# A new hand-written order for a gated attention and expert kernel: single output matmuls, squares moved between engines, stores and copies at other places

## The chip, the cores and the metric

The kernel runs on one NeuronCore of a Trainium2 chip. The core has five engines that run side by side and meet through semaphores: TensorE (PE, matmuls; its weight loads, PEld, overlap them), VectorE (DVE), ScalarE (ACT), GpSimd (POOL) and SyncE (SP, which here only issues DMAs). The metric is the device time of one execution in microseconds (us). Before the change the median of three runs is 221.41 us (220.65 to 221.46).

## The reference, cut to what matters

Inputs are x (8 batches, 8 heads, 512 rows, 64 columns), state (8, 8, 32, 64), w_in (512 x 2048), w_out (2048 x 512) and alpha (2048). Per batch and head two cross attentions are made, then a layer with the activation h + sin(alpha h)^2 / alpha runs over all rows:

```python
scores = scale * x @ state.T;   a = softmax(scores);   xread = a @ state
scores2 = scale * state @ x.T;  a2 = softmax(scores2); sread = a2 @ x
rows = concat([xread, sread], axis=2)        # 544 rows a batch, heads side by side: 4352 x 512
h = rows @ w_in
s = sin(alpha * h)
g = h + s * s / (alpha + 1e-9)
out = g @ w_out                              # 4352 x 512, float32
```

Inside, matmul operands are bfloat16; the sums are float32.

## The kernel before, in words

**Tiles.** The 512 rows of x of one batch are one unit t = 0 to 7; the 256 rows of all the state reads are a ninth unit, t = 8. The 2048 columns between the two big matmuls are cut into 16 tiles f of 128. `xread @ w_in` is not made in two steps: for each batch the kernel first makes M = state @ w_in per head (`m`, in four slices s and two head groups g, each a PSUM tile that `me` copies out as bfloat16), and then h = A M, where A is the softmax (`h`: two 512-column matmuls per f; for the first batch `hg`, one matmul of the two each). For t = 8 `h` is four 256-column matmuls on `xs_all`.

**One f tile.** `h` fills a PSUM bank; `si` (ScalarE) takes the sine; `sq` squares it, on ScalarE (A), VectorE (V) or GpSimd (G); `gt` (VectorE) adds h and frees the bank, leaving the tile gT. Then `o` multiplies gT with a tile of w_out into the output tile of 128 rows `st` (four per batch, 16 matmuls of 512 columns in each). `oc` copies the finished output tile to an `o_sb` buffer (six of them), `os` stores it from SP's queue.

**The attention of a batch.** `lx` loads x of a batch as bfloat16, issued by GpSimd; `pk` (VectorE, in two halves) copies it into another arrangement; `td` transposes it by a DMA on SP's queue (for batch 1, `xt` on TensorE); `sc` makes the scores, `ex` the exponent, `rs`, `rr` sum and reciprocal, `nm` (GpSimd) the product A, `ad` transposes A by DMA on SP's queue into AT, which `h` needs. `w`, `cs`, `rc`, `xs` make the state's read into `xs_all`. A change between exponent and sine makes ScalarE load a table.

**Loads at the start.** x of batch 0 comes in four parts by SP (`lq`); GpSimd issues state (`l_st`), w_in in four parts (`li`), w_out in four (`lo`) and x of the next batches (`lx`).

**What sets the order.** Nothing is scheduled by a machine: `ORDER` (lines 21 to 155) is a list of step names, and the kernel calls the method of each in turn, under a manual schedule. So each engine runs its own instructions in the order of that list, and each DMA queue too; a step that must wait holds up whatever stands behind it on its engine. The parts of a step's name are its arguments: `sq.3.7.V` is batch 3, f 7, on VectorE; `o.0.3.2.3` is batch 0, output rows 3, f from 2 up to 3. The order also names the PSUM bank of each tile (`h.1.2.5`: bank 5). The eight banks hold one tile each, so a tile in a bank can start only when the reader of the last one is done. `warm_up` steps are matmuls on zeros that no result uses.

The loop that plays the list is

```python
for step in ORDER:
    name, *args = step.split(".")
    getattr(steps, name)(*(int(a) if a.isdigit() else a for a in args))
```

Of the kernel before, what the change touches and what calls it, by code (L numbers as in the profile page):

```python
# [13 lines left out]
FP32 = mybir.dt.float32  # L14
# [31 lines left out]
si.0.12 o.0.0.10.11 o.0.3.9.11 sq.0.13.G ad.1 hg.0.15.0.2 sq.0.12.A o.0.1.10.12 hg.0.15.1 gt.0.12
o.0.2.8.10 si.0.15 o.0.2.10.11 gt.0.13 o.0.0.11.12 hg.0.14.0.4 sq.0.15.A hg.0.14.1 o.0.3.11.13
si.0.14 gt.0.15 o.0.0.12.13 o.0.1.12.13 o.0.3.13.14 sq.0.14.A pk.2.0.V o.0.1.13.14 pk.2.1.V h.1.2.5
gt.0.14 h.1.4.6 td.2 si.1.2 lx.3.0.1 h.1.0.2 si.1.4 o.0.0.13.15 sq.1.2.V h.1.1.4 si.1.0 gt.1.2
sq.1.4.G o.0.3.14.16 si.1.1 o.0.2.11.13 sq.1.0.A oc.0.3.V h.1.6.5 sq.1.1.G gt.1.4 o.0.2.13.14 os.0.3  # L50
h.1.3.0 si.1.6 gt.1.0 o.0.1.14.16 si.1.3 sq.1.6.G h.1.13.6 gt.1.1 oc.0.1.A o.0.2.14.15 o.0.0.15.16
si.1.13 h.1.15.2 sq.1.3.G lx.4.0.1 gt.1.6 os.0.1 o.0.2.15.16 oc.0.0.A h.1.5.4 sq.1.13.V oc.0.2.V
si.1.15 h.1.7.3 os.0.0 gt.1.3 o.1.1.0.1.5 si.1.5 os.0.2 h.1.8.1 sq.1.15.G gt.1.13 o.1.1.1.2 si.1.7
o.1.2.0.2.7 sq.1.5.A o.1.1.2.3 sq.1.7.G h.1.12.0 gt.1.15 si.1.8 h.1.9.6 gt.1.5 o.1.2.2.3 si.1.12
sq.1.8.G o.1.2.3.5 gt.1.7 si.1.9 o.1.1.3.4 h.1.10.2 sq.1.12.A pk.3.1.V h.1.11.4 sq.1.9.G gt.1.8
o.1.2.5.6 si.1.10 o.1.2.6.7 gt.1.12 h.1.14.3 si.1.11 sq.1.10.G o.1.2.7.8 gt.1.9 sc.2.1.1 si.1.14
o.1.1.4.7 sq.1.11.A pk.3.0.V sq.1.14.G o.1.1.7.8 gt.1.10 td.3 o.1.2.8.9 sc.2.0.0 o.1.1.8.9 gt.1.11
o.1.1.9.10 ex.2.0 o.1.3.0.2.6 gt.1.14 o.1.3.2.4 o.1.2.9.10 o.1.3.4.5 o.1.2.10.12 ex.2.1 o.1.2.12.13
rs.2.0 o.1.1.10.11 m.2.2.2.4.3.0 rr.2.0 rs.2.1 o.1.2.13.14 nm.2.0.0.4.G me.2.3.0.A o.1.2.14.15 w.0.1
rr.2.1 me.2.2.1.A me.2.3.1.V o.1.3.5.6 nm.2.1.0.4.G me.2.2.0.A o.1.3.6.7 o.1.2.15.16 cs.0 oc.1.2.A  # L60
m.2.0.3.4.0.2 ad.2 rc.0 o.1.3.7.8 me.2.1.1.A o.1.3.8.9 sc.3.0.7 xs.0.1 me.2.1.0.A o.1.1.11.12 os.1.2
me.2.0.0.V sc.3.1.2 me.2.0.1.A o.1.1.12.13 o.1.3.9.10 xs.0.0 pk.4.1.V pk.4.0.V td.4 o.1.3.10.11
ex.3.0 o.1.1.13.16 ex.3.1 rs.3.0 o.1.3.11.13 oc.1.1.A o.1.3.13.14 rr.3.0 h.2.0.0 rs.3.1 nm.3.0.0.4.G
os.1.1 o.1.3.14.16 si.2.0 rr.3.1 h.2.1.3 oc.1.3.V nm.3.1.0.4.G h.2.2.4 h.2.8.1 os.1.3 h.2.3.7 ad.3
si.2.2 o.1.0.0.3.2 si.2.8 sq.2.0.V o.1.0.3.4 sq.2.2.G gt.2.0 h.2.4.5 si.2.1 o.1.0.4.6 si.2.3
sq.2.8.G o.1.0.6.7 gt.2.2 h.2.9.6 si.2.4 o.2.3.0.1.0 o.1.0.7.8 sq.2.1.G o.1.0.8.9 sq.2.3.A gt.2.8
o.1.0.9.10 h.2.5.4 si.2.9 gt.2.3 o.1.0.10.11 sq.2.4.G o.1.0.11.12 si.2.5 h.2.7.1 gt.2.1 o.1.0.12.13
sq.2.9.A sq.2.5.G o.1.0.13.14 gt.2.4 o.1.0.14.15 si.2.7 o.1.0.15.16 o.2.0.0.1.7 gt.2.9 o.2.0.1.2
oc.1.0.A h.2.6.3 sq.2.7.G gt.2.5 o.2.3.1.2 os.1.0 o.2.3.2.3 si.2.6 h.2.10.5 o.2.3.3.4 sq.2.6.A
# [88 lines left out]
class Steps:  # L158
# [372 lines left out]
    def h(k, t, f, bank):  # L531
# [9 lines left out]
        else:  # L541
            for q in range(k.Q):
# [3 lines left out]
                )  # L546


    def hg(k, t, f, g, *bank):
        if g == 0:  # L550
            k.t["h", t, f] = k.ps(bank[0], [k.P, k.S], FP32, "h_ps")
        k.nc.tensor.matmul(  # L552
# [28 lines left out]
    def o(k, t, st, f0, f1, *bank, half=None):  # L581
        cols = k.cols(half)
# [81 lines left out]
```

## Time and profile before

| | |
|---|---|
| median of the runs | 221.41 us |
| the profiled execution | 221.22 us, span 219.2 us |
| PE busy | 211.4 us, 96% |
| VectorE busy | 162.9 us, 74% |
| ScalarE busy | 173.4 us, 79% |
| GpSimd busy | 106.2 us, 48% |
| chain that ended last | PE 90%, DMA 6% |
| `gt` (L576), 512 columns | 128 times, mean 742 ns |
| `si` (L560), 512 columns | 128 times, mean 695 ns |
| square on GpSimd / ScalarE / VectorE (L201, L569, L201) | mean 1045 / 640 / 449 ns |
| `pk` (L348) | 14 times, mean 429 ns |
| x loads (L275) | 7, median 7.5 us from issue to landing |

The page and the trace come from one execution. Times in it count from the start of its span. A duration is longer than an instruction's share of its engine, since the next one starts before the last has drained; where it matters, the distance from start to start is named. Idle time of an engine that the last chain does not run through costs nothing.

### The profile page before, as it was taken

The page shows a single profiled execution, that of the slowest core. Times are in us where ns is not written, and L with a number is a line of the kernel's source. Part 1 is how long each engine was busy: PE and PEld are TensorE (multiplying, and loading weights), DVE is VectorE, ACT ScalarE, POOL GpSimd, SP SyncE. Part 2 cuts the span into 40 slices and gives each one's busy share as a digit, 9 for nine tenths or more (in the row PEclk, how much of TensorE's full clock was granted, in tenths as well). Part 3 has the DMA queues.
Part 4 walks back from the last instruction along what each step waited for, and adds up shares of the span by engine and source line. Part 5 has one row for each costly group of instructions (what it writes and reads, how often), then busy time and mean ns, then how long its engine had stood idle before and what let it go on. Part 6 is the DMA issues. An engine that isn't in the chain of part 4 may idle for free.

```text
span 219.2 us, 4303 instructions
## 1 busy us (share of the span) xinstructions
PE 211.4 (96%) x1593; PEld 104.5 (48%) x1619; DVE 162.9 (74%) x287; ACT 173.4 (79%) x297; POOL 106.2 (48%) x114
## 2 busy tenths in 40 slices
PE   7989999999999999999999999999999999999994
PEld 3744544444444534444454444454445555665452
DVE  3769996999787789989888788888667987661201
ACT  4799778997998979898996999798848896785111
POOL 5959533895195647753943387273501082121000
PEclk9999999999999999999999999999999999999999
DMA  6999999987491029167145327470220211012042
GB/s 195 178 206 204 205 204 146 217 169 133 101 238 48 3 92 143 57 144 96 48 79 131 109 71 96 134 110 0 48 100 0 98 48 48 0 51 96 1 143 96
DMA packets 38052, 23.48 MB, mean 107 GB/s; under 512 B 20992, under 2 KB 33680, under 8 KB 38032
## 3 DMA queue, kind: packets, MB, share of 16 engines
q1 hardware_dynamic: 26128, 15.08, 26.5%
q0 software_dynamic: 11648, 8.13, 26.0%
q8 instruction: 12, 0.20, 0.3%
q14 instruction: 8, 0.07, 0.1%
q10 hardware_dynamic: 256, 0.01, 0.1%
HBM read 17.44 MB, written 8.91 MB: 120 GB/s over the span
## 4 chain that ended last, share of the span: by engine, by line
PE 90%; DMA 6%; POOL 1%; issue 1%; ACT 0%
PE o_ps L587 54%; PE h_ps L537 22%; DMA w_in_sb<-in_moe_w_in_dram 5%; PE m_ps L488 4%; PE h_ps L543 3%; PE h_ps L552 2%; PE w_ps L450 2%; PE s_ps L399 2%; PE w_ps L461 1%; DMA s<-in_state_dram 1%; POOL w_in_sb L282 1%; PE x_ps L376 0%; POOL st_nat L267 0%; POOL s01b L255 0%; ACT o_sb L595 0%
## 5 line engine op out<-in xcount | busy, mean ns | idle before, releaser
L587 PE MATMUL o_ps<-w_out_sb,gT 128*128 128x512 bf16 (+2 forms) x542 | 133.9, 373 | 1.6 <-issue 1.0
L576 DVE SCALAR_TENSOR_TENSOR gT<-s,inva_sb,h_ps 128x512 bf16<-128x512 bf16 (+1 forms) x144 | 96.8, 713 | 20.4 <-POOL s L201 10.8
L201 POOL TENSOR_TENSOR s<-s 128x512 bf16<-128x512 bf16 (+1 forms) x75 | 75.9, 1022 | 64.4 <-ACT s L560 62.7
L560 ACT ACTIVATE s<-h_ps,alpha_sb 128x512 bf16<-128x512 f32 (+1 forms) x144 | 88.8, 670 | 11.1 <-PE h_ps L543 4.5
L587 PEld LDWEIGHTS <-gT 128*128 128x128 bf16 x560 | 52.3, 98 | 60.3 <-issue 5.0
L537 PE MATMUL h_ps<-AT,M 128*128 128x512 bf16 x219 | 60.0, 379 | 0.3
L537 PEld LDWEIGHTS <-M 128*128 128x128 bf16 x224 | 21.7, 98 | 25.9 <-issue 0.4
L569 ACT ACTIVATE s<-s 128x512 bf16<-128x512 bf16 (+1 forms) x53 | 31.4, 594 | 0.8
L201 POOL TENSOR_TENSOR A<-E,rR 128x512 bf16<-128x512 bf16 x16 | 16.6, 1056 | 23.8 <-ACT o_sb L595 12.9
L595 ACT COPY o_sb<-o_ps 128x512 f32<-128x512 f32 (+2 forms) x24 | 13.7, 570 | 16.6 <-PE o_ps L587 16.5
L496 ACT CAST M<-m_ps 128x512 bf16<-128x512 f32 x35 | 18.6, 594 | 8.2 <-PE m_ps L488 8.2
L496 DVE CAST M<-m_ps 128x512 bf16<-128x512 f32 x29 | 18.9, 679 | 2.5 <-PE m_ps L488 2.1
L595 DVE COPY o_sb<-o_ps 128x512 f32<-128x512 f32 x11 | 7.5, 685 | 12.9 <-PE o_ps L587 12.9
L201 DVE TENSOR_TENSOR s<-s 128x512 bf16<-128x512 bf16 (+1 forms) x16 | 7.0, 439 | 6.2 <-ACT s L560 6.1
L410 DVE TENSOR_REDUCE R<-E 128x16 f32<-128x512 bf16 x16 | 10.4, 657 | 0.7 <-ACT E L406 0.6
L488 PE MATMUL m_ps<-w_in_sb,stT 64*32 64x512 bf16 x256 | 10.2, 382 | 0.1
L468 DVE RECIPROCAL rC<-w_ps 128x128 f32<-128x128 f32 x8 | 7.6, 948 | 3.3 <-PE w_ps L461 3.2
L303 PE MATMUL warm_ps<-warm 128*128 128x128 bf16 (+3 forms) x66 | 8.6, 271 | 1.4 <-DVE warm L209 1.2
L552 PE MATMUL h_ps<-AT,M 128*128 128x512 bf16 x29 | 8.4, 379 | 0.9 <-ACT M L496 0.7
L406 ACT ACTIVATE E<-s_ps 128x512 bf16<-128x512 f32 x16 | 8.8, 602 | 0.4 <-PE s_ps L399 0.4
L543 PE MATMUL h_ps<-xs_all,w_in_sb 128*128 128x256 bf16 x64 | 9.1, 273 | 0.0
L543 PEld LDWEIGHTS <-w_in_sb 128*128 128x128 bf16 x64 | 6.3, 98 | 3.4
(56 smaller groups left out, 101.8 us busy)
## 6 DMA issues: line engine op xcount, KB each, us to landing
out_dram<-o_sb SPq DMA_DIRECT2D x33, 256.0 KB, 2.3
xnat<-in_x_dram POOLq DMA_DIRECT2D x7, 512.0 KB, 7.5
w_in_sb<-in_moe_w_in_dram POOLq DMA_DIRECT2D x4, 512.0 KB, 10.9
w_out_sb<-in_moe_w_out_dram POOLq DMA_DIRECT2D x4, 512.0 KB, 18.0
x<-in_x_dram SPq DMA_DIRECT2D x4, 256.0 KB, 4.2
st_nat<-in_state_dram POOLq DMA_DIRECT2D x1, 256.0 KB, 5.3
out_dram<-o_sb SPq DMA_DIRECT2D x1, 192.0 KB, 1.9
s<-in_state_dram SPq DMA_DIRECT2D x1, 128.0 KB, 2.2
```

The lines of the kernel that those rows point to most:

```text
L201: {"V": k.nc.vector, "G": k.nc.gpsimd}[eng].tensor_tensor(out, a, b, ALU.mult)
L410: k.nc.vector.reduce_sum(R[:, g], k.t["E", b][:, g].rearrange("p c (h j) -> p (c h) j", j=k.Ns), axis=AX.X)
L488: k.nc.tensor.matmul(k.t["m", b, s + n, g][o0:o0 + k.Ns, :], k.stT[k.half(r), b * k.G + g, c0:c0 + k.Ns], k.w_in_sb[k.half(r), 2 * g + h, ...
L496: k.copy(eng)(k.t["M", b][:, g, s * k.FW:(s + 1) * k.FW], k.t["m", b, s, g][:])
L537: k.nc.tensor.matmul(hp[:, :n], k.t["M", t][:, g, fs], k.t["AT", t][:, g, :], start=(g == 0), stop=(g == k.G - 1),)
L543: k.nc.tensor.matmul(hp[:, :n], k.w_in_sb[:, q, fs], k.xs_all[:, q].rearrange("p b j -> p (b j)"), start=(q == 0), stop=(q == k.Q - 1),)
L552: k.nc.tensor.matmul(k.t["h", t, f][:], k.t["M", t][:, g, f * k.P:(f + 1) * k.P], k.t["AT", t][:, g, :], start=(g == 0), stop=(g == k.G - 1),)
L560: k.nc.scalar.activation(s[:, :n], k.t["h", t, f][:, :n], ACT.Sin, scale=k.alpha_sb[:, f:f + 1])
L569: k.nc.scalar.activation(s2[:, :n], s[:, :n], ACT.Square)
L576: k.nc.vector.scalar_tensor_tensor(gT[:, :n], k.t["s2", t, f][:, :n], k.inva_sb[:, f:f + 1], k.t["h", t, f][:, :n], ALU.mult, ALU.add,)
L587: k.nc.tensor.matmul(k.t["o", t, st, half][:, cols], k.t["gT", t, f][:, rows], k.w_out_sb[:, f, cols], start=(f == 0), stop=(f == k.FT - 1),)
L595: k.copy(eng)(o_sb[:, cols], k.t["o", t, st, half][:, cols])
```

## The change

The list is replaced as a whole by another order of the same work, and two methods are cut finer so that the list can say more. `hg` no longer takes a bank: `ho` takes it, and the two matmuls of a tile can come in either order. `o` is one matmul, and `oo` takes its bank; the 16 matmuls of an output tile can come in any order of f, each tile's first matmul starts the sum and its 16th ends it (`k.made` counts them). `m` steps are listed one slice at a time.

What the list changes besides, counted from the two lists: squares go from 53 / 16 / 75 on ScalarE / VectorE / GpSimd to 46 / 55 / 43; copies of M (`me`) from 35 / 29 on ScalarE / VectorE to 38 / 26; three of the four casts of batch 0's x (`xq`) from ScalarE to VectorE; the warm-up matmuls from 66 to 15. The stores `os` stand at other places of SP's queue, some well behind their `oc`: `os.1.0` to `os.1.3` come in one run behind `os.2.3`. The two halves of `pk` are apart for most batches, and `pk.3.1.V` and `pk.5.1.V` stand earlier among VectorE's steps. The last piece of the output is `oh.7.3.0` (384 columns) instead of `oh.7.3.1` (128 columns).

```diff
@@ the order (before): its start, the steps around pk.3 and pk.5, its end
-touch_x l_s01 consts touch lq.0.S ident_ l_alpha lq.1.S zero.0 warm_up.7.512.3 exp_table lq.2.S
...
-sq.1.8.G o.1.2.3.5 gt.1.7 si.1.9 o.1.1.3.4 h.1.10.2 sq.1.12.A pk.3.1.V h.1.11.4 sq.1.9.G gt.1.8
...
-os.2.2 h.3.3.0 gt.3.4 oc.2.1.A h.3.12.2 si.3.3 pk.5.1.V o.3.2.0.1.7 os.2.1 m.4.2.1.3.5.6 pk.5.0.V
...
-oc.7.0.A o.7.2.2.5 os.7.0 o.7.2.5.11 oh.7.3.0.1 o.7.2.11.13 och.7.3.0.A o.7.2.13.15 osh.7.3.0
-o.7.2.15.16 oh.7.3.1.4 oc.7.2.V os.7.2 och.7.3.1.A osh.7.3.1
@@ the order (after): its start, the steps around pk.3.1 and pk.5.1, the stores of batch 1, its end
+touch_x l_s01 consts touch lq.0.S ident_ l_alpha lq.1.S zero.0 warm_up.5.512.7 exp_table lq.2.S
...
+o.0.2.13 o.0.0.13 o.0.0.14 o.0.0.15 pk.1.1.V o.0.3.13 o.0.1.14 oo.1.3.1 lx.3.0.1 h.1.0.5 oc.0.0.A
+si.1.0 pk.2.0.V h.1.14.6 o.0.3.15 si.1.14 o.0.2.14 o.0.2.15 oc.0.2.A h.1.6.0 si.1.6 sq.1.14.G
+pk.2.1.V td.2 oc.0.3.V sq.1.6.G o.0.1.13 o.0.1.15 oc.0.1.A os.0.1 h.1.4.4 si.1.4 h.1.7.2 si.1.7
+sq.1.7.G oo.1.2.7 sq.1.0.V gt.1.0 o.1.3.0 o.1.2.0 pk.3.1.V h.1.9.3 h.1.2.5 gt.1.14 o.1.2.14 o.1.3.14
...
+si.3.14 sq.3.14.V gt.3.14 o.2.0.3 h.3.10.2 si.3.10 sq.3.10.A gt.3.10 gt.3.8 o.2.2.13 lx.5.0.1
+pk.5.1.V o.2.2.8 o.2.2.2 h.3.0.5 si.3.0 sq.3.0.V o.2.2.3 h.3.11.0 si.3.11 o.2.0.7 o.2.0.8 oc.2.0.A
...
+sq.3.11.A gt.3.11 gt.3.6 si.3.12 sq.3.12.G o.2.1.4 gt.3.12 o.2.1.1 h.3.5.4 o.2.1.3 os.1.1 os.1.2
+h.3.2.5 os.1.3 o.3.3.15 os.1.0 si.3.5 sq.3.5.G gt.3.5 o.2.2.1 si.3.2 h.3.3.0 si.3.3 sq.3.3.G ad.4
...
+oc.8.0.V os.8.0 o.7.2.15 o.7.1.0 o.7.2.11 o.7.2.8 o.7.2.13 o.7.2.7 oh.7.3.1.0 o.7.2.0 o.7.2.6
+och.7.3.1.V oc.7.2.V os.7.2 o.7.1.1 o.7.1.3 o.7.1.15 oc.7.1.A os.7.1 oh.7.3.0.0 osh.7.3.1
+och.7.3.0.A osh.7.3.0
@@ the methods
-        k.t = {}
+        k.t, k.made = {}, {}
...
-    def hg(k, t, f, g, *bank):
-        if g == 0:
-            k.t["h", t, f] = k.ps(bank[0], [k.P, k.S], FP32, "h_ps")
+    def ho(k, t, f, bank):
+        k.t["h", t, f] = k.ps(bank, [k.P, k.S], FP32, "h_ps")
+        k.made["h", t, f] = 0
+
+    def hg(k, t, f, g):
+        k.made["h", t, f] += 1
         k.nc.tensor.matmul(
             k.t["h", t, f][:], k.t["M", t][:, g, f * k.P:(f + 1) * k.P], k.t["AT", t][:, g, :],
-            start=(g == 0), stop=(g == k.G - 1),
+            start=k.made["h", t, f] == 1, stop=k.made["h", t, f] == k.G,
         )
...
-    def o(k, t, st, f0, f1, *bank, half=None):
+    def oo(k, t, st, bank, half=None):
+        k.t["o", t, st, half] = k.ps(bank, [k.P, k.DOUT], FP32, "o_ps")
+        k.made["o", t, st, half] = 0
+
+    def o(k, t, st, f, half=None):
         cols = k.cols(half)
-        if f0 == 0:
-            k.t["o", t, st, half] = k.ps(bank[0], [k.P, k.DOUT], FP32, "o_ps")
         rows = slice(st * k.P, (st + 1) * k.P) if t < k.B else slice(st, k.B * k.Ns, 2)
-        for f in range(f0, f1):
-            k.nc.tensor.matmul(
-                k.t["o", t, st, half][:, cols], k.t["gT", t, f][:, rows],
-                k.w_out_sb[:, f, cols], start=(f == 0), stop=(f == k.FT - 1),
-            )
+        k.made["o", t, st, half] += 1
+        k.nc.tensor.matmul(
+            k.t["o", t, st, half][:, cols], k.t["gT", t, f][:, rows], k.w_out_sb[:, f, cols],
+            start=k.made["o", t, st, half] == 1, stop=k.made["o", t, st, half] == k.FT,
+        )
...
     def oh(k, t, st, half, bank):
-        k.o(t, st, 0, k.FT, bank, half=half)
+        k.oo(t, st, bank, half=half)
+        for f in range(k.FT):
+            k.o(t, st, f, half=half)
```

## The prediction

> **What bounds the kernel now.** I read the page first (share of each engine, chain that ended last), then the busy times by stretch, then who waits for whom, then the loads one by one.
>
> ```profile
> span 219.2 us, 4303 instructions
> PE 211.4 (96%) x1593; PEld 104.5 (48%) x1619; DVE 162.9 (74%) x287; ACT 173.4 (79%) x297; POOL 106.2 (48%) x114
> ...
> PE 90%; DMA 6%; POOL 1%; issue 1%; ACT 0%
> ```
>
> TensorE (PE) is busy in 96% of the span and 90% of the chain that ended last. The 6% of DMA is the wait for the third part of w_in at the start. By stretch (columns: length, then busy time and count of PE, weight loads, VectorE, ScalarE, GpSimd):
>
> ```profile
> 0.00:17.40 17.40, 14.71 (x186) 8.76 (x187) 9.86 (x25) 12.77 (x23) 12.59 (x22) 1.00 1.01 194
> ...
> 216.00:219.20 3.20, 0.12 (x3) 0.00 (x0) 0.00 (x0) 0.27 (x1) 0.00 (x0) 1.00 0.31 110
> ...
> 17.40:216.00 198.60, 196.53 (x1407) 95.78 (x1432) 153.04 (x263) 160.41 (x274) 93.62 (x93) 1.00 0.49 99
> ```
>
> From 17.4 us, when that part lands, to 216 us PE is busy for 196.5 of 198.6 us. Asked what PE waited for from 20 to 216 us, the trace names one thing:
>
> ```profile
> PE o_ps L587 <- issue: 1.0, 6, 0.2
> ```
>
> So no other engine holds PE up now. The time is a head of 17.4 us set by DMA, a PE part with almost nothing to win, and a tail of 3.2 us. The profiled execution took 221.22 us for its span of 219.2; the median of the runs shown is 221.41 (220.65 to 221.46). My sum is made against 221.22.
>
> **The change part by part.** *TensorE's work.* The matmuls are the same but for warm-ups (66 before, 15 after), which lie in the head. I add the steps of either order from the first `m` on w_in's third part (17.4 us) with what the trace shows from start to start: 216 ns for a 512-column matmul, 0.325 us for an `m` pair of tiles, 0.24 `sc`, 0.46 `xt` and `w`, 0.30 `cs`. Before: 776 full matmuls and the rest, end at 214.9 (the trace: 216.1; 17 stretches of `m` with some 0.09 us at each turn are not in it). After: 773 and the same rest. Three `hg` matmuls more stand ahead of that `m`, in a stretch where PE waits for w_in anyway: **-0.65 us**. Bounds: 0 if `hg` comes late there, -0.65 if all three fit. I take -0.65, since `m` for w_in's first part starts at 11.87 and 11 `hg` need 2.4 of the 5.5 us up to 17.4. The runs of adjacent `m` steps number 17 in both orders, so splitting the `m` steps costs nothing.
>
> *Single matmuls instead of runs, started in any order* (`ho`, `oo`, `o` with one f): each matmul has its own weight load in both kernels (98 ns beside 216), so nothing by itself; the present trace already holds `o_ps` and `h_ps` matmuls taking turns at 216 ns.
>
> *The tail.* The last piece was 128 columns (matmul 219 ns, copy 265, 64 KB store 1.8 us). It becomes the 384-column piece (326, 478, 192 KB 1.9 us): **+0.4 us**.
>
> *The head.* Three of four x casts go from ScalarE (618 ns each) to VectorE, `inva` comes later, warm-ups thin out. All of it lies before the first `m` at 11.87 us, which waits for w_in (issued behind the same GpSimd steps in both orders): nothing; a chain late by one cast, 0.6 us, would still leave 2.5 us of room up to 17.4.
>
> *Squares.* GpSimd does 43 instead of 75, VectorE 55 instead of 16, ScalarE 46 instead of 53. VectorE gains 35 full squares at 0.345 us from start to start (12.1), 4 half ones (0.8), three x casts (about 1.3), and loses three `me` (1.8): about +13 us beside 45.6 us of idle time from 17.4 to 216. Its total is not the bound. GpSimd loses 32 us and ScalarE some 4, off the path.
>
> ```profile
> L201 DVE TENSOR_TENSOR s<-s x16: 285/424/658, 15.1 to 192.4; 128x512 bf16<-128x512 bf16 x15, 128x256 bf16<-128x256 bf16 x1
>   POOL s L201: 10.8, 24
> ```
>
> Of 15 full squares on VectorE two (578 and 658 ns) ran longer beside a GpSimd step. With 2 in 15 of 39 added ones, that is 5 times 0.2 us, 1 us of VectorE's time and none of PE's unless it falls at a tight place; on the other side VectorE's 10.8 us of waits behind GpSimd's squares shrink. Zero on PE's path, bounds 0 and +1.
>
> [...]
>
> *Where x loads meet VectorE.* This is what I hold decisive. `lx.b` is issued by GpSimd, `pk.b` copies the landed tile on VectorE, in order with the `gt` steps that PE needs. Issues and, in order, the microseconds from issue to landing of each:
>
> ```profile
> 33.97 0.94 POOL L275 DMA_DIRECT2D xnat<-in_x_dram  x1
> 43.36 0.94 POOL L275 DMA_DIRECT2D xnat<-in_x_dram  x1
> ...
> 81.50 0.94 POOL L275 DMA_DIRECT2D xnat<-in_x_dram  x1
> ...
> 98.94 0.94 POOL L275 DMA_DIRECT2D xnat<-in_x_dram  x1
> ```
> ```profile
> xnat<-in_x_dram POOLq DMA_DIRECT2D x1, 512.0 KB, 7.3
> xnat<-in_x_dram POOLq DMA_DIRECT2D x1, 512.0 KB, 8.2
> xnat<-in_x_dram POOLq DMA_DIRECT2D x1, 512.0 KB, 7.5
> xnat<-in_x_dram POOLq DMA_DIRECT2D x1, 512.0 KB, 5.6
> ```
> ```profile
> 47.51 0.41 DVE L348 COPY xp<-xnat 128x1024 bf16<-128x1024 bf16 x1
> ...
> 92.74 0.75 DVE L348 COPY xp<-xnat 128x1024 bf16<-128x1024 bf16 x2
> ```
>
> A load alone takes 5.6 us; beside a DMA transpose 7.3 and 7.5, beside stores 8.2. Today the copies come 13.5 us (batch 3) and 11.2 us (batch 5) after the issue, so nothing waits. The new order pulls both forward:
>
> - Batch 3: `lx.3` follows `sq.0.15.G`. PE's sum ends `h.0.15` at 32.3, ScalarE's sine after it takes 0.9, the square 1.0: issue at 34.3. `pk.3.1.V` now stands right behind `gt.1.0`: `h.1.0` ends at 37.8, sine 0.9, VectorE's `oc.0.3`, square and `gt` bring it to 40.2. The landing goes as in the same place now (7.3, beside `td.2`): 41.6. Behind it waits `gt.1.14`, and PE wants it for `o.1.2.14` at 41.9 (101 full matmuls after 17.4, and 2.7 us of others). Landing plus copy 0.34, `gt` 0.74 and 0.1 of signals is 42.8: **+0.9 us**. At 5.6 us the load lands at 39.9 and costs nothing; at 8.2 it costs 1.8.
> - Batch 5: `sc.4.1` ends at 77.4; exponent 0.8, sum and reciprocal 0.9, two GpSimd products 2.1: `lx.5` at 81.3, as now. But `pk.5.1.V` moves from behind `gt.3.4` to behind `gt.3.10` and `gt.3.8`, which VectorE ends at 86.7. Beside the load stand five stores in one run (`os.2.3`, then `os.1.1`, `1.2`, `1.3`, `1.0`, held behind it on SP's queue) and `ad.4`. The nearest row is the load beside stores, 8.2: landing at 89.5. Behind the copy wait `sq.3.0`, `gt.3.0`; PE's `h.3.2.5` at 89.1 needs the bank that `gt.3.0` frees. 89.5 + 0.34 + 0.35 + 0.74 + 0.1 = 91.0: **+1.9 us**. At 5.6 us (86.9) it costs nothing; at 9 us 2.7.
> - Batches 6 and 7: `lx.6` at 99.2 with no store near, 5.6 us, lands at 104.8; VectorE reaches the copy at 105.2. `lx.7` at 132 lands at 137.6, the copy at 138.7. Nothing, 2 us at most for batch 6 if it took 8.2.
>
> [...]
>
> *Waits and stores moved on SP.* Stores go late and in bunches; six `o_sb` buffers rotate, and each tile's store stands ahead of the sixth tile after it by 10 us or more of PE time: nothing, bounds 0 and +0.5. The transposes keep their reserve: last `sc` to first `h` is 7.8 us for batch 2 (8.8 before) and 8.5 for batch 5, of which exponent, sums, two products and a 3.0 us transpose need 6.3.
>
> *Sum:* 221.22 - 0.65 + 0.4 + 0.9 + 1.9 = 223.8. I predict **223.7**.
>
> **The rivals.** *Not slower: the loads land in time.* One mechanism at these two places: at 6.3 us or less from issue to landing neither copy delays PE. For it: two of the later loads took 5.6; stores may be over before the load's packets start. Against it: 7.3, 7.5 and 8.2 were measured where transposes and stores ran beside. Price: 221.22 - 0.65 + 0.4 = 221.0. If only batch 3 waits: 221.9.
>
> *The new order does what it says and its reserve is gone.* Between the last `o` of an output tile and the next matmul in its bank stood at least five matmuls (1.08 us), middle 1.94; now four (0.86), middle 1.29, where copy (588 ns), drain and signals need 0.85. From an `h` to the first `o` on it with a GpSimd square in between: middle 9.9 us before, 5.6 now. If each of some 20 such places ran 0.1 us late, 2 us: 223 without the loads, 225.7 with them. Against it: several places of today's order have as little, and PE never waited over 0.2 us.
>
> *The clock.* Seven 512-column warm-ups begin the kernel at 427 ns each, half speed; from 5.4 us on matmuls run at full speed. With 15 instead of 66 PE idles more up to 17.4. If the speed falls at 11 us, `m` and 11 `hg` take twice 3.9 us and overrun: +0.65 for the gain and up to 1.5 more, 223.1 without the loads. Against it: PE is never idle for over about a microsecond.
>
> **How the numbers follow.** Both loads late 0.55 (223.7, own range 222.6 to 224.9); only batch 3, 0.14 (221.9); neither, 0.18 (221.0); reserve or clock on top, 0.13 (225 to 226). About 0.5% is what a measurement of this kernel tells from no change: 220.3 to 222.5 by the median. Slower: 0.55 + 0.13 = 0.68. Faster needs more than the head can give, 0.07 out of the 0.18; same the rest, 0.25. Range 220.7 to 225.3.
>
> **What would show it.** Right: VectorE waiting at L350 (`pk`) for `xnat` near 41 and 88 us, PE gaps just behind them, five stores in a row near 82, `lx.5` over 7 us; PE's first full stretch with three more `hg` before 17.4; a last copy of 384 columns. Wrong: no wait at `pk`, or PE gaps elsewhere, at bank changes or in the first 17 us.

## The result and the profile after

The changed kernel takes **229.45 us** (median of 6 runs, 228.16 to 230.29) against 221.30 for the kernel before beside it (6 runs, 220.65 to 221.46): a ratio of 1.037 with a 95% interval of 1.033 to 1.041. Slower was forecast, but the size was not: 8 us instead of 2.3. The profiled execution, one of the two fastest of the six, took 228.51 us for a span of 226.4; the sum below is made against that and the 221.22 of before, so it explains 7.3 of the 8 us between the medians.

The page of the changed kernel (span, PE's busy share and the granted clock in 40 slices, the chain that ended last):

```profile
span 226.4 us, 4152 instructions
...
PE   6979999999999999299999999999999999999993
...
PEclk9999999999999999979999999999999999999998
...
PE 76%; DVE 9%; DMA 6%; ACT 5%; issue 2%; POOL 0%; SPq 0%
```

PE carried 90% of the last chain; now it carries 76%, and its row has a 2 in the slice from 90.6 to 96.2 us (each slice is 5.66 us); in the next slice, up to 101.9 us, the row of the clock has a 7. So I cut the span around that place (length, then busy time and count of PE, weight loads, VectorE, ScalarE, GpSimd, then the granted clock):

```profile
17.85:90.20 72.35, 71.57 (x525) 33.33 (x534) 63.77 (x115) 64.82 (x107) 32.43 (x32) 1.00 0.73 129
90.20:98.70 8.50, 3.96 (x12) 1.51 (x12) 4.43 (x8) 2.83 (x5) 3.18 (x4) 0.81 0.57 90
98.70:223.00 124.30, 123.07 (x870) 61.53 (x884) 97.28 (x177) 92.05 (x157) 26.29 (x27) 1.00 0.31 77
```

On both sides PE is 99% busy at full clock. In the 8.5 us between, it works for less than half of the time, at a clock of 0.81. Who waited for whom, from 20 us on (one line of PE's answer, one of VectorE's):

```profile
PE h_ps L539 <- DVE gT L581: 4.5, 1, 4.5
```
```profile
DVE xp L350 <- DMA xnat<-in_x_dram: 4.6, 1, 4.6
```

This is the chain that the prediction named for batch 5: the copy `pk.5.1` waits for the load `lx.5`, behind it stands `gt.3.0`, and PE's `h.3.2.5` needs the bank that `gt.3.0` frees. The second place, batch 3, does not show at all in this execution. SP's queue and the transfers issued between 80 and 95 us (last column: microseconds from issue to landing):

```profile
82.22 2.69 SPq L609 DMA_DIRECT2D out_dram<-o_sb  x5
85.02 2.94 SPq L442 DMA_TRANSPOSE AT<-A  x1
```
```profile
out_dram<-o_sb SPq DMA_DIRECT2D x6, 256.0 KB, 6.0
xnat<-in_x_dram POOLq DMA_DIRECT2D x1, 512.0 KB, 10.4
AT<-A SPq DMA_TRANSPOSE x1, 8.9
```

The five stores in a run are there, and the load issued at 82.88 us beside them takes 10.4 us. Before, the same load took 7.5 and the transpose 6.7. VectorE and PE at the place (start, time until the end of the group):

```profile
86.63 2.06 DVE L581 SCALAR_TENSOR_TENSOR gT<-s,inva_sb,h_ps 128x512 bf16<-128x512 bf16 x3
93.32 0.43 DVE L350 COPY xp<-xnat 128x1024 bf16<-128x1024 bf16 x1 [4.62 <-DMA xnat<-in_x_dram]
93.66 0.42 DVE L203 TENSOR_TENSOR s<-s 128x512 bf16<-128x512 bf16 x1
94.11 3.38 DVE L581 SCALAR_TENSOR_TENSOR gT<-s,inva_sb,h_ps 128x512 bf16<-128x512 bf16 x5
```
```profile
89.78 0.59 PE L539 MATMUL h_ps<-AT,M 128*128 128x512 bf16 x2
94.92 0.59 PE L539 MATMUL h_ps<-AT,M 128*128 128x512 bf16 x2 [4.54 <-DVE gT L581]
95.35 0.93 PE L594 MATMUL o_ps<-w_out_sb,gT 128*128 128x512 bf16 x2
96.07 1.06 PE L539 MATMUL h_ps<-AT,M 128*128 128x512 bf16 x2
96.92 2.86 PE L594 MATMUL o_ps<-w_out_sb,gT 128*128 128x512 bf16 x8
```

The pause is one part of the loss. The other stands in the last lines: two matmuls of 512 columns took 0.59 us before the pause and take 1.06 after it, eight take 2.86 where they would take 1.89. From start to start the trace has 427 ns for seven in a row from 95.64 us on and 344 for an eighth, as for the warm-ups at the very start (427); then it is 216 again.

**A measure for the rest.** For each group of `m` matmuls I take its start in the trace minus its place in the sum of PE's steps (the durations of the prediction, zero at 17.4 us). What grows in this number is time that PE lost. It is worked out from the start times in the traces of all kernels of this study, one execution each; read along a row, and down for what a change did:

| kernel, us lost up to | 17.4 | 30.5 | 54 | 79 | 100 | 125 | end |
|---|---|---|---|---|---|---|---|
| before | 0.01 | 0.43 | 0.54 | 0.76 | 0.78 | 0.89 | 1.17 |
| after | 0.45 | 0.80 | 1.05 | 1.33 | 7.58 | 7.69 | 8.68 |
| e1_copy_late | -0.03 | 0.32 | 1.92 | 2.20 | 2.29 | 3.35 | 4.34 |
| e2_stores_early | 0.45 | 0.80 | 1.05 | 1.33 | 6.64 | 6.74 | 7.73 |
| e3_zeros_in_wait | -0.09 | 0.26 | 0.51 | 0.78 | 5.54 | 5.65 | 6.64 |
| e4_before_copy_early | 0.37 | 0.79 | 0.90 | 1.12 | 7.17 | 7.24 | 7.56 |
| e5_both_late | 1.69 | 2.97 | 3.95 | 4.18 | 4.26 | 5.32 | 6.31 |
| e6_small_piece_last | 0.06 | 0.41 | 1.39 | 1.62 | 1.71 | 2.77 | 3.77 |
| e7_more_warm_ups | 0.36 | 0.71 | 1.69 | 1.93 | 2.01 | 3.08 | 4.08 |
| e9_eight_zeros | 0.05 | 0.40 | 1.99 | 2.27 | 7.09 | 7.19 | 8.19 |
| e10_both_in_slack | -0.34 | 0.01 | 1.42 | 1.67 | 1.75 | 1.86 | 2.86 |
| e11_slack_and_warm | -0.12 | 0.23 | 1.65 | 1.89 | 1.98 | 2.20 | 3.20 |
| e12_squares_off_gpsimd | -0.38 | -0.03 | 1.30 | 1.53 | 1.61 | 1.88 | 2.87 |
| e13_copy_on_scalar | 0.01 | 0.36 | 1.32 | 1.56 | 1.64 | 1.74 | 2.74 |

In all rows but those of before and of e4 the sum itself is 0.65 us shorter. Of the 7.17 us by which the span grew, 6.25 arise between 79 and 100 us (7.58 less 1.33), against 0.02 before.

### The profile page after: what moved, and what is told of

It is laid out like the page before. It is cut to its first block, busy times and chain, and to the rows that moved or that the text cites. A ratio compares the mean times of both kernels' runs of the same rounds, so it can differ in the third digit from the quotient of the medians.

```text
span 226.4 us, 4152 instructions
## 1 busy us (share of the span) xinstructions
PE 213.6 (94%) x1540; PEld 103.9 (46%) x1568; DVE 177.5 (78%) x327; ACT 171.2 (76%) x289; POOL 74.5 (33%) x82
## 4 chain that ended last, share of the span: by engine, by line
PE 76%; DVE 9%; DMA 6%; ACT 5%; issue 2%; POOL 0%; SPq 0%
PE o_ps L594 44%; PE h_ps L539 17%; DMA xnat<-in_x_dram 5%; DVE gT L581 4%; PE h_ps L557 3%; PE m_ps L490 3%; PE h_ps L545 3%; PE s_ps L401 2%; ACT s L565 2%; DMA x<-in_x_dram 1%; DVE s L203 1%; DVE rC L470 1%; DVE M L498 1%; PE w_ps L452 1%; PE x_ps L363 1%
## 5 line engine op out<-in xcount | busy, mean ns | idle before, releaser
L594 PE MATMUL o_ps<-w_out_sb,gT 128*128 128x512 bf16 (+2 forms) x542 | 138.5, 376 | 1.6 <-issue 0.5
L565 ACT ACTIVATE s<-h_ps,alpha_sb 128x512 bf16<-128x512 f32 (+1 forms) x144 | 90.4, 668 | 20.8 <-PE h_ps L539 13.0
L203 POOL TENSOR_TENSOR s<-s 128x512 bf16<-128x512 bf16 (+1 forms) x43 | 44.2, 1035 | 99.3 <-ACT s L565 93.5
L539 PE MATMUL h_ps<-AT,M 128*128 128x512 bf16 x216 | 62.3, 381 | 4.6 <-DVE gT L581 4.5
L203 DVE TENSOR_TENSOR s<-s 128x512 bf16<-128x512 bf16 (+1 forms) x55 | 22.5, 411 | 8.4 <-ACT s L565 8.1
L574 ACT ACTIVATE s<-s 128x512 bf16<-128x512 bf16 (+1 forms) x46 | 27.2, 592 | 0.9
L602 ACT COPY o_sb<-o_ps 128x512 f32<-128x512 f32 (+1 forms) x22 | 12.8, 586 | 16.8 <-PE o_ps L594 16.7
L498 DVE CAST M<-m_ps 128x512 bf16<-128x512 f32 x26 | 16.9, 674 | 1.1 <-PE m_ps L490 0.9
L602 DVE COPY o_sb<-o_ps 128x512 f32<-128x512 f32 (+1 forms) x13 | 8.4, 653 | 6.6 <-PE o_ps L594 6.4
L350 DVE COPY xp<-xnat 128x1024 bf16<-128x1024 bf16 x14 | 6.0, 438 | 4.7 <-DMA xnat<-in_x_dram 4.6
L557 PE MATMUL h_ps<-AT,M 128*128 128x512 bf16 x31 | 8.5, 380 | 0.5 <-ACT M L498 0.5
## 6 DMA issues: line engine op xcount, KB each, us to landing
w_in_sb<-in_moe_w_in_dram POOLq DMA_DIRECT2D x4, 512.0 KB, 10.4
```

Source lines behind the costliest of these rows:

```text
L203: {"V": k.nc.vector, "G": k.nc.gpsimd}[eng].tensor_tensor(out, a, b, ALU.mult)
L498: k.copy(eng)(k.t["M", b][:, g, s * k.FW:(s + 1) * k.FW], k.t["m", b, s, g][:])
L539: k.nc.tensor.matmul(hp[:, :n], k.t["M", t][:, g, fs], k.t["AT", t][:, g, :], start=(g == 0), stop=(g == k.G - 1),)
L557: k.nc.tensor.matmul(k.t["h", t, f][:], k.t["M", t][:, g, f * k.P:(f + 1) * k.P], k.t["AT", t][:, g, :], start=k.made["h", t, f] == 1, sto ...
L565: k.nc.scalar.activation(s[:, :n], k.t["h", t, f][:, :n], ACT.Sin, scale=k.alpha_sb[:, f:f + 1])
L574: k.nc.scalar.activation(s2[:, :n], s[:, :n], ACT.Square)
```

## The experiments

The first four were compared with the kernel before at 221.37 us, e5 to e9 at 221.38, e10 and e11 at 221.56, the last two at 221.57; a ratio is always to that, with its 95% interval.

**e1_copy_late: does it all hang on the place of pk.5.1?**

```diff
-... gt.3.8 o.2.2.13 lx.5.0.1 pk.5.1.V o.2.2.8 ... oc.2.2.A os.2.2 pk.5.0.V td.5
+... gt.3.8 o.2.2.13 lx.5.0.1 o.2.2.8 ... oc.2.2.A os.2.2 pk.5.1.V pk.5.0.V td.5
```

> The changed kernel with one step moved: pk.5.1.V goes from behind gt.3.8 to just ahead of pk.5.0.V, where the order before has it. Theory A (the copy that waits 4.6 us for lx.5's landing, PE's 4.5 us wait behind it and ten matmuls at half speed after that are the loss): PE loses neither, so 228.5 - 4.7 - 1.7 = 222.1 for a profiled execution, median 221.5 to 223, no VectorE wait for xnat, no 427 ns matmuls after 90 us. Rival B (the order has lost its reserve everywhere and this wait is only where it shows first): the lost time turns up at other steps, 225 or more.

223.96 us (222.78 to 224.52), ratio 1.0104 (1.0067 to 1.0140): one step moved takes away 5.5 of the 8 us. The load still takes 10.5 us and the five stores still run beside it, but nothing waits for it; PE goes through 90 us without a pause and no matmul is slow. So the late load costs only through the copy that stands in VectorE's order. What is left shows at another place: in this execution `lx.3` landed 6.4 us after its issue instead of 5.9, VectorE came to the copy at 40.80 us instead of 41.19, and VectorE and PE read

```profile
41.07 1.13 DVE L350 COPY xp<-xnat 128x1024 bf16<-128x1024 bf16 x1 [0.27 <-DMA xnat<-in_x_dram]
42.12 0.74 DVE L581 SCALAR_TENSOR_TENSOR gT<-s,inva_sb,h_ps 128x512 bf16<-128x512 bf16 x1
42.78 0.94 DVE L203 TENSOR_TENSOR s<-s 128x512 bf16<-128x512 bf16 x1
```
```profile
42.92 0.61 PE L594 MATMUL o_ps<-w_out_sb,gT 128*128 128x512 bf16 x2 [0.51 <-DVE gT L581]
43.36 0.59 PE L539 MATMUL h_ps<-AT,M 128*128 128x512 bf16 x2
44.56 0.39 PE L594 MATMUL o_ps<-w_out_sb,gT 128*128 128x512 bf16 x1 [0.61 <-DVE gT L581]
```

The wait for the load is only 0.27 us. But the copy, 0.42 us elsewhere, takes 1.13 and the square behind it 0.94, both beside a GpSimd square; together with the wait PE loses 1.4 us (start to start 0.67 and 0.77 over the matmul). In the profiled execution of the changed kernel the same copy came at 41.19, waited for nothing and took 0.48.

**e2_stores_early: are the five stores what makes the load late?**

```diff
-ad.3 h.2.13.2 ... os.2.3 ... os.1.1 os.1.2 h.3.2.5 os.1.3 o.3.3.15 os.1.0
+ad.3 os.1.1 os.1.2 os.1.3 os.1.0 h.2.13.2 ... os.2.3 ... h.3.2.5 o.3.3.15
```

> The changed kernel with the four stores os.1.1, 1.2, 1.3 and 1.0 moved ahead of os.2.3 on SP's queue, right behind ad.3, so that they are issued near 67 us, long before lx.5; the copy stays where the change put it. If the run of stores makes lx.5 land late (10.4 us in the changed kernel): lx.5 lands in 7.5 us beside ad.4 as in the kernel before, 2.9 us earlier, PE waits some 1.6 us instead of 4.5 and keeps its clock: 228.5 - 2.9 - 1.7 = 223.9, median 223.5 to 225. If ad.4 alone makes it late: lx.5 stays near 10 us and the time near 229.

227.41 us (225.85 to 229.75), ratio 1.0243 (1.0199 to 1.0287). The load and the transpose, with one store ahead of them instead of five (one more follows at 88.90 us in both kernels):

```profile
xnat<-in_x_dram POOLq DMA_DIRECT2D x1, 512.0 KB, 7.8
AT<-A SPq DMA_TRANSPOSE x1, 6.8
```

From 10.4 to 7.8 us: 2.6 us of the late landing come from the four stores moved. The time gains only 2 us, for two reasons that one sees in VectorE's and PE's lines:

```profile
90.69 1.27 DVE L350 COPY xp<-xnat 128x1024 bf16<-128x1024 bf16 x1 [2.00 <-DMA xnat<-in_x_dram]
91.88 1.25 DVE L203 TENSOR_TENSOR s<-s 128x512 bf16<-128x512 bf16 x1
```
```profile
93.97 0.59 PE L539 MATMUL h_ps<-AT,M 128*128 128x512 bf16 x2 [3.59 <-DVE gT L581]
...
95.26 3.58 PE L594 MATMUL o_ps<-w_out_sb,gT 128*128 128x512 bf16 x8
```

Where VectorE waits 2.6 us less, it now meets GpSimd's squares, and copy and square take 2.5 us where they took 0.85. And a pause of 3.6 us still brings the slow matmuls (eight in 3.58 us).

**e3_zeros_in_wait: what do the slow matmuls cost by themselves?** Sixteen matmuls of zeros are added into an open output tile, which leaves the result as it is, just where PE waits.

```diff
-os.1.1 os.1.2 h.3.2.5
+os.1.1 os.1.2 z.2.1.16 h.3.2.5
```

> The changed kernel with 16 matmuls of zeros that add nothing, put on PE just ahead of h.3.2 into the open output tile of batch 2, rows 1, so that PE works for 3.5 of the 4.7 us in which it waited; the wait itself ends no earlier. If the idle time makes the clock fall and that is a part of the loss of its own: the ten matmuls at 427 ns are gone, 1.7 us in the profiled execution (226.8) and up to 3 in others, median 226 to 227.5. If the slow matmuls have another cause: 229 as the changed kernel.

226.43 us (226.33 to 228.76), ratio 1.0255 (1.0194 to 1.0316).

```profile
89.88 3.62 PE L617 MATMUL o_ps<-warm 128*128 128x512 bf16 x16
94.56 0.59 PE L539 MATMUL h_ps<-AT,M 128*128 128x512 bf16 x2 [1.07 <-DVE gT L581]
94.99 0.59 PE L594 MATMUL o_ps<-w_out_sb,gT 128*128 128x512 bf16 x2
95.42 0.59 PE L539 MATMUL h_ps<-AT,M 128*128 128x512 bf16 x2
95.86 1.89 PE L594 MATMUL o_ps<-w_out_sb,gT 128*128 128x512 bf16 x8
```

VectorE waits as long as ever (4.8 us) and PE does nothing useful in that time, but the matmuls after it run at full speed. In the table the stretch from 79 to 100 us costs 4.76 instead of 6.25, so the slow clock is 1.5 us of the profiled loss. The medians are 3.0 us apart; in the two profiled executions another 0.5 us lies in the head, which has nothing to do with the zeros.

**e4_before_copy_early: does the old order do the same?** The kernel before, with the one step moved.

```diff
-... gt.3.2 o.2.2.7.8 ... si.3.3 pk.5.1.V o.3.2.0.1.7 ...
+... gt.3.2 pk.5.1.V o.2.2.7.8 ... si.3.3 o.3.2.0.1.7 ...
```

> The kernel before with one step moved: pk.5.1.V goes from behind gt.3.4 forward to right behind gt.3.2, where VectorE comes at 84.6 us; lx.5 landed at 89.0 there with no run of stores beside it. Theory A: VectorE waits 4.4 us for xnat, gt.3.0 ends at 90.2, PE's h.3.9 waits 3.4 us for the bank: 221.3 + 3.4 = 224.7, and 226 if the clock falls too. Rival B (the place of one copy matters only where reserve is short all round): the reserve of the order before takes up most of it, under 222.5.

226.84 us (224.86 to 227.94), ratio 1.0231 (1.0168 to 1.0293). VectorE waits 3.7 us for a load that takes 7.5 as in the kernel before, and (PE)

```profile
90.53 0.59 PE L537 MATMUL h_ps<-AT,M 128*128 128x512 bf16 x1 [3.02 <-DVE gT L576]
91.33 1.06 PE L537 MATMUL h_ps<-AT,M 128*128 128x512 bf16 x2 [0.22 <-DVE gT L576]
```

Twelve matmuls at 427 ns follow. The pause and the fall of the clock behind it need nothing else of the new order: 5.5 us of loss come from one step moved in the old one. The clock did not fall each time: one of the four executions (224.86 us) has a granted clock of 0.999, the other three (226.06 to 227.94 us) 0.985 to 0.992. The same holds for e2: one of four, 225.85 us, at 1.000, the others, 227.28 to 229.75 us, at 0.984 to 0.991.

**e5_both_late, e6_small_piece_last, e7_more_warm_ups: the rest.**

```diff
 e5: e1, and
-o.1.3.0 o.1.2.0 pk.3.1.V h.1.9.3 ... gt.1.1 pk.3.0.V
+o.1.3.0 o.1.2.0 h.1.9.3 ... gt.1.1 pk.3.1.V pk.3.0.V
 e6: e5, and
-oh.7.3.1.0 ... och.7.3.1.V ... oh.7.3.0.0 osh.7.3.1 och.7.3.0.A osh.7.3.0
+oh.7.3.0.0 ... och.7.3.0.V ... oh.7.3.1.0 osh.7.3.0 och.7.3.1.A osh.7.3.1
 e7: e6, and
-warm_up.5.512.7 ... warm_up.1.512.7 xtq.0.3 ... warm_up.1.416.7 ... xtq.3.4
+warm_up.7.512.7 ... warm_up.2.512.7 xtq.0.3 ... warm_up.2.512.7 ... warm_up.2.128.7 xtq.3.4
```

> The changed kernel with both moved copies put back late: pk.5.1.V just ahead of pk.5.0.V (as in e1_copy_late, 223.96 us) and pk.3.1.V just ahead of pk.3.0.V. Theory (the two copies are what the change costs, and the rest lies at the two ends): in e1_copy_late TensorE lost 0.67 us at 42.0 and 0.77 at 43.6 behind pk.3.1.V and the square beside GpSimd, 1.4 together; both go, 222.5 us. Rival (the order has no reserve left, and what pk.3.1.V no longer loses another step does): 223.5 to 224.0, with new gaps of TensorE between 42 and 54 us.

> As e5_both_late, and the two pieces of the last tile change places: 384 columns first, 128 columns last, as in the kernel before. Theory: the tail behind TensorE's last matmul goes from 3.4 to 3.1 us, so 0.3 us less than e5_both_late, about 222.2 us. Rival (the store's fixed part hides the copy's length): the same as e5_both_late within 0.1.

> As e6_small_piece_last, with five more warm-up matmuls of 512 columns in the head (7 for 5 at the start, one more ahead of the first and one more ahead of the third transpose of x) and two of 128. Theory (the head lost its gain to a clock that came up later): the score matmuls at 8.0 us take 0.40 us for 0.63, the first m starts near 11.9 instead of 12.4 and the third group of m near 17.4 instead of 17.85; 0.45 us less than e6_small_piece_last, about 221.8. Rival (the head is bound by VectorE and GpSimd, whose first normalisation starts only at 10.4 us, or by the third w_in part, which lands at 17.3): the m groups stay where they are within 0.15 and the time is that of e6_small_piece_last.

224.18 us (ratio 1.0141, 1.0099 to 1.0183), 223.87 (1.0123, 1.0085 to 1.0162) and 224.12 (1.0139, 1.0109 to 1.0169): three misses. All are where e1 was. The reasons differ:

- e5: the pauses at 42 and 43.6 us are gone, and another has come, 0.74 us where the second scores of batch 2 (`sc.2.1`) wait for a `gt`. From 30.5 to 54 us e6, the same order there, loses 0.98 us for e1's 1.60. The profiled execution of e5 also shows what made it take 226.12 us where others took 223.5: w_in came late, and PE waited for its second part (line below). In that execution the four parts took 12.0 us in the median instead of 10.4.
- e6: PE's last matmul ends 3.7 us before the span does, not 3.1. In the kernel before the last four stores were issued over 7.0 us; here, as in the changed kernel, SP's queue gets its last four close together (over 1.8 us, from 217.3 on; 3.4 us there), and the small piece has to follow the others.
- e7: the scores at 8 us run at full speed, but begin at 8.48 instead of 8.00, behind the matmuls added, and the first `m` starts at 12.25.

```profile
16.32 0.61 PE L490 MATMUL m_ps<-w_in_sb,stT 64*32 64x512 bf16 x10 [1.29 <-DMA w_in_sb<-in_moe_w_in_dram]
```

One miss told more than it was made for. In e1, e5, e6 and e7 the table has a new loss of 1.0 us between 100 and 125 us that the changed kernel does not have. In e6 it is here (VectorE, then PE):

```profile
94.98 1.60 DVE L350 COPY xp<-xnat 128x1024 bf16<-128x1024 bf16 x2
```
```profile
97.23 0.40 PE L490 MATMUL m_ps<-w_in_sb,stT 64*32 64x512 bf16 x6 [0.18 <-DVE M L498]
```

Put late, the two copies stand right ahead of the evictions of the next M, one of them again stretched to 1.26 us beside a GpSimd square, and PE waits for the banks.

**e9_eight_zeros: how short must the pause be?**

```diff
-z.2.1.16 h.3.2.5
+z.2.1.8 h.3.2.5
```

> The changed kernel with 8 matmuls of zeros, which add nothing to the result, ahead of h.3.2.5 in place of the 16 of e3_zeros_in_wait: TensorE then stands about 3.0 us (4.7 less 8 times 0.216) instead of 1.2. Theory 1 (a pause of 3.0 us is already enough for the clock to fall, as the pauses of 3.2 to 4.7 us were): ten matmuls at 427 ns behind it, and some 2 us more than e3_zeros_in_wait. Theory 2 (3.0 us is short enough): matmuls at 216 ns right behind the pause, and a time like that of e3_zeros_in_wait, 226.4.

228.01 us in its one execution. The pause is there and the slow matmuls are not:

```profile
91.37 1.89 PE L617 MATMUL o_ps<-warm 128*128 128x512 bf16 x8
96.11 0.59 PE L539 MATMUL h_ps<-AT,M 128*128 128x512 bf16 x2 [2.85 <-DVE gT L581]
...
97.40 1.89 PE L594 MATMUL o_ps<-w_out_sb,gT 128*128 128x512 bf16 x8
```

From 79 to 100 us it loses 4.82 us, as e3 does (4.76). That the time is nevertheless 1.6 us over e3's median is for the most part batch 3: its `lx.3` took 6.9 us, and the table has 1.59 us from 30.5 to 54 where e3, with 5.8 us, has 0.25. So in the executions traced a pause of 2.85 us kept the clock, and pauses of 3.02 (e4), 3.59 (e2) and 4.54 lost it. The length alone need not decide that. For e4, the traced 227.62 us less the 2.5 us of its twelve slow matmuls (12 times 0.211) make an estimated 225.1, about the 224.86 us of the execution that kept its clock, so the pause there, which was not traced, can have been as long.

The traces show when the clock changed. In the changed kernel it rises at 10.13 us, falls at 95.47, rises at 98.88 and falls again, behind the last matmul, at 225.17 us; these changes lie 85.33, 3.41 and 126.29 us apart, which is 25, 1 and 37 times 3.413. In the kernel before it rises at 5.40 us and falls at 220.44, behind the end of the span, 215.04 us or 63 times 3.413 later. In e4 it falls at 89.52 us, 2.0 us into the pause, and stays low for twice 3.41 us. The stretch ahead of the fall and the one behind it (length, PE's busy time and count, granted clock) read in the changed kernel and in e4

```profile
92.05:95.47 3.42, 0.55 (x3) 1.00 0.64 128
95.47:98.88 3.41, 3.41 (x10) 0.50 0.00 0
```
```profile
86.11:89.52 3.41, 1.40 (x7) 1.00 0.82 108
89.52:92.93 3.41, 2.19 (x5) 0.50 0.00 0
```

In the 3.41 us ahead of a fall PE had worked for 0.55 us (changed kernel) and 1.40 (e4); in e2 it worked for 1.29 us of the 3.41 us ahead of its slow matmuls, from the end of the pause at 93.97 to 95.26 us. In e9 the pause of 2.85 us leaves at most 0.56 us of work in 3.41 us around it, about as little as in the changed kernel, and the clock stayed. So the work in 3.41 us does not decide by itself. What does, the length of the pause or the moment at which it comes, is not shown: no run put a pause of the same length at another time.

**e10_both_in_slack, e11_slack_and_warm: the copies where VectorE has room.**

```diff
 e10
-pk.3.1.V h.1.9.3 h.1.2.5 gt.1.14 o.1.2.14 o.1.3.14 sq.1.4.V gt.1.4 h.1.13.6
+h.1.9.3 h.1.2.5 gt.1.14 o.1.2.14 o.1.3.14 sq.1.4.V gt.1.4 pk.3.1.V h.1.13.6
-lx.5.0.1 pk.5.1.V ... os.2.2 pk.5.0.V td.5 ... o.3.0.0 gt.3.13
+lx.5.0.1 ... os.2.2 ... o.3.0.0 pk.5.1.V pk.5.0.V td.5 gt.3.13
 e11: e10, and
-warm_up.5.512.7 ... warm_up.1.512.7 xtq.0.3
+warm_up.7.512.7 ... xtq.0.3
```

> The changed kernel with the copies of x put where VectorE was seen to have room: pk.5.1.V, pk.5.0.V and td.5 behind the evictions of the next batch's M, ahead of gt.3.13 (VectorE stood 1.06 us there in e6_small_piece_last), and pk.3.1.V two squares later than in the changed kernel, behind gt.1.4. Theory (what is left of the loss in e1 to e7 is what a late copy does to VectorE where it stands: 0.9 us at 97 us, 0.9 at 52 to 54, 1.4 at 42 where it stands early): all three go, 222.0 to 222.3 us, loss of TensorE at the m groups near 119 us about 1.3 for 2.8 in e6. Rival (the order has no reserve, so that 0.4 us of copy costs as much wherever it stands): 223.5 to 224.

> As e10_both_in_slack, with seven warm-up matmuls for five at the start and none between the transposes of s01 and of x, so that TensorE works nearly without a gap up to 5.1 us. Theory (the clock that comes up late costs 0.45 us in some executions): scores at 0.40 us for eight, the first m at 11.9 us or before, in every execution; 0.1 to 0.4 us less than e10. Rival (the head is set by VectorE and GpSimd): the first m at 11.9 to 12.4 as before and the time of e10 within 0.1.

223.24 us (222.68 to 225.17, ratio 1.0083, 1.0055 to 1.0110) and 223.40 (1.0085, 1.0051 to 1.0118). Half right: the loss between 79 and 125 us is down to 0.19 us (0.13 before), but from 30.5 to 54 us it is 1.41. There the copy met GpSimd's squares again:

```profile
42.59 0.82 DVE L350 COPY xp<-xnat 128x1024 bf16<-128x1024 bf16 x1
43.34 1.39 DVE L581 SCALAR_TENSOR_TENSOR gT<-s,inva_sb,h_ps 128x512 bf16<-128x512 bf16 x2
44.65 1.16 DVE L203 TENSOR_TENSOR s<-s 128x512 bf16<-128x512 bf16 x1
```

The head's clock gives nothing that shows in e11: its scores ran at 0.40 us for eight, but so did they in this execution of e10.

**e12_squares_off_gpsimd, e13_copy_on_scalar: is it GpSimd that stretches VectorE's steps?**

```diff
 e12: e10, and
-sq.1.7.G ... sq.1.13.G
+sq.1.7.A ... sq.1.13.A
 e13: e10, and
-pk.3.1.V
+pk.3.1.A
```

> As e10_both_in_slack, with the two GpSimd squares that stood beside VectorE's copy of x at 42.6 us and beside its square at 44.65 us (sq.1.7 and sq.1.13) done by ScalarE. Theory (VectorE's step is stretched by a GpSimd step that runs at the same time: 0.82 for 0.42 us and 1.16 for 0.42 us): the copy and the square take 0.42 us each, TensorE's pauses of 0.68 us at 43.2 and 0.77 us at 45.7 shrink to 0.3 or less each, the loss at the m group near 54 us goes from 1.4 to about 0.4, time 222.2 us. Rival 1 (the load's DMA writes, not GpSimd, stretch the copy): copy and square stay at 0.8 and 1.2 us. Rival 2 (1.2 us more on ScalarE make it the late one): the steps are short, but TensorE's pauses stay, behind ScalarE; 223.2 or more.

> As e10_both_in_slack, with the copy pk.3.1 done by ScalarE and the GpSimd squares left as they were. Theory (the stretched copy on VectorE is half of what is lost in the third batch): VectorE gains 0.82 us at 42.6, the pause at 43.2 goes, the one at 45.7 behind the stretched square stays; the copy takes ScalarE about 1.1 us (a copy of 512 columns took 0.59), time 222.6. Rival (ScalarE has no room between 40.7 and 43.8, where it runs without idling): TensorE waits for ScalarE's squares and sigmoids in place of VectorE, 223.2 or more.

223.24 us (ratio 1.0069, 1.0041 to 1.0096) and 222.97 (1.0070, 1.0040 to 1.0101). VectorE's steps of e10 again, in e12:

```profile
42.54 0.42 DVE L350 COPY xp<-xnat 128x1024 bf16<-128x1024 bf16 x1
...
44.19 0.42 DVE L203 TENSOR_TENSOR s<-s 128x512 bf16<-128x512 bf16 x1
...
47.53 0.75 DVE L581 SCALAR_TENSOR_TENSOR gT<-s,inva_sb,h_ps 128x512 bf16<-128x512 bf16 x1 [0.81 <-ACT s L574]
```

0.82 and 1.16 us became 0.42 and 0.42: the stretching is GpSimd's doing. The time did not move, since VectorE now waits for ScalarE's square at 47.5 and PE stands 0.53 us behind it there. In e13 ScalarE's copy took 1.04 us and PE's pause moved to 46.8 (0.62 us, VectorE behind GpSimd). No version of the new order reached the time of the kernel before; the nearest are 1.4 us above it.

## Why the prediction was wrong, by its steps

| step | predicted | profiled after | shown by |
|---|---|---|---|
| three more `hg` in the head | -0.65 | -0.65, and +0.44 of clock in this execution | table, e1, e3, e4 |
| batch 3, `pk.3.1` | +0.9 | +0.1 (1.5 in e1 and e9) | e1, e9 |
| batch 5, `pk.5.1`: the pause | +1.9 | +4.7 | e1, e2 |
| batch 5: slow matmuls behind it | not priced | +1.5 | e3, e9 |
| from 125 us on | 0 | +0.7 | table alone |
| tail | +0.4 | +0.3 | trace, e6 |
| sum | 2.6 | 7.2 of span | |

The middle column is the difference of the two kernels' rows in the table; 0.1 us more comes and goes in the stretches not named.

**The step that failed is the landing of `lx.5`, "the nearest row is the load beside stores, 8.2".** The mechanism was right to the instruction: which copy, which `gt`, which bank, which matmul, which stores. What was wrong is how the rows were used. I had 5.6 us for a load alone, 7.5 beside a transpose, 8.2 beside stores, and forecast both a transpose and stores beside this one; I took the larger of the two disturbances where they were to come together. Measured were 10.4 us. e2, with the transpose and one store ahead of the load, has 7.8, so the stores are worth 2.6 as in the row of 8.2; 5.6 + 1.9 + 2.6 = 10.1 would fit. That the transpose adds 1.9 is not shown, though: no run took it away, and `lx.3`, beside `td.2` in every version of the new order, took anything from 5.8 (e3) to 6.9 us (e9). My upper bound of 9 us was too low for the same reason.

The pause became 4.7 us instead of 1.9. Of the 2.8 us, 2.2 are the longer load; the rest is that `lx.5` was issued 1.6 us later than in my sum (82.88 for 81.3) while PE came to `h.3.2` only some 1.1 us later (90.2 for 89.1).

**The step that was missing is the clock behind the pause.** The rival on the clock was there, but I looked for it in the head, where PE idles often and briefly (0.65 us at most in the changed kernel once its first matmul has run); the pause that I forecast myself was 1.9 us, and no run has one of that length; the longest that is seen to keep the clock is 2.85 (e9). The price does not grow evenly with the pause: where the clock falls, 1.5 us (the changed kernel against e3) and more (2.5 in e4) are added at once. The traces show 427 ns for 216, over 3.41 us in the changed kernel and twice that in e4, and slow matmuls that begin at no fixed distance behind the pause (with the fourth in the changed kernel, the seventh in e2, the second at the latest in e4). PE had worked for 0.55 to 1.40 us of the 3.41 us ahead of them, and 3.02 us of pause by the trace could be enough. The upper end of my own range for the pause (2.7 us at 9 us of landing) lies only 0.3 us below that.

**Batch 3** went as its bounds said, though the row taken from the same place (7.3 us) did not carry over (5.9), and "at 6.3 us or less neither copy delays PE" was a good line: with 5.8 and 5.9 us (e3, after) the stretch costs 0.25 us, with 6.4 and 6.9 (e1, e9) 1.6. Which one comes differs from execution to execution. What I had not seen is that the wait itself is the smaller part (0.27 us in e1, 0.82 in e9) and that in e1 most of the cost is the copy and a square stretched beside GpSimd.

**VectorE's steps beside GpSimd's** I priced at "bounds 0 and +1" with squares in mind. The stretching is real (in e12 0.82 and 1.16 us became 0.42 and 0.42), and it hits the copies, which I took at 0.34 us from start to start (0.42 as a duration): they lasted 1.13 in e1, 1.27 in e2, 1.26 in e6, stretches of up to 0.85 us beside GpSimd's squares of 1.04. By what means GpSimd stretches them is not shown.

**The head.** The gain of 0.65 us is there: in e1, e3, e6 and e13 PE arrives at the third `m` group as early as before, with 0.65 us more work done. The 0.45 us in the profiled execution goes with a clock that comes up later (at 10.13 us, in the kernel before at 5.40): the second eight scores, from 9.3 us on, take 390 ns from first to last start, where they take 213 in e1. e4, in the old order with all its warm-ups, lost 0.37 us at the same place: the place varies in both.

**Reserve.** From 125 us to the end every version of the new order loses 1.0 us and the old 0.28, in stops of 0.1 to 0.2 us at changes of kind. That is not the rival's mechanism: the loss is the same to 0.01 us in all of them, and from 20 us on PE's whole answer on the changed kernel names one wait for another engine, the 4.5 us above. Where the rival holds is from 30.5 to 54 us, once the copies are moved: each repair (e5 to e13) brought another engine to the front. For e10 the account closes: +1.30 from 30.5 to 54 us, +0.72 from 125 on and +0.32 in the tail, -0.65 by the sum, -0.35 up to 17.4 and +0.02 elsewhere make the 1.4 us by which its span is longer. Why the old order has reserve there where the new one has none, and which stops from 125 us on are the order's own, is not settled.

## What to carry to other kernels

A load that nothing waits for may take as long as it likes (10.5 us in e1, without a wait behind it); once a step that waits for it is pulled forward in an engine's order, price the landing by all the transfers in flight beside it, not by the slowest row seen so far: here it was 5.6 us alone (batch 6 before), 7.8 beside a transpose and one store (e2), 10.4 beside the transpose and five stores. When the forecast is a pause of TensorE, see whether its upper end can cost the clock as well, since the price jumps there: here a pause of 3.02 us did in the traced execution, one of 2.85 did not, and one of the four executions of the kernel with 3.02 (e4) kept its clock. And when VectorE takes work from GpSimd, look which of its steps, plain copies too, will run beside GpSimd's: each such meeting cost up to 0.85 us here, beside a GpSimd step of 1.04.

## What the runs showed of the hardware that was not expected

- A load of 512 KB by GpSimd's queue took 5.6 to 6.0 us in batches 6 and 7; in batch 5 it took 7.5 to 7.8 beside a DMA transpose and 10.2 to 10.7 beside the transpose and five stores of 256 KB, and the transpose went from 6.7 to 8.9 at the same time.
- In the traces pauses of PE of 3.02, 3.59 and 4.54 us were each followed by eight to twelve matmuls at or near 427 ns, pauses of 2.85 us and less by none. In the traces of the two kernels the clock's changes lie 3.41, 85.33, 126.29 and 215.04 us apart, whole multiples of 3.413. Matmuls of zeros in the pause kept the clock up, and the stretch cost 4.76 us instead of 6.25 (e3).
- A copy of 128 x 1024 bfloat16 on VectorE takes 0.42 us, and up to 1.27 beside GpSimd's squares; the same copy on ScalarE took 1.04 us.
